# Leaky relu of the first block by ScalarE and GpSimd, VectorE in program order in the last four experts, gates copied by GpSimd

## The chip, the cores and the metric

The kernel runs on one core of a Trainium2 chip. The core has five engines, each with a queue of its own that it works off in order: TensorE (PE; its weight loads are shown apart as PEld), VectorE (DVE), ScalarE (ACT), GpSimd (POOL) and SyncE (SP), which here issues nearly all DMAs. The metric is the device time of one execution in microseconds, the median of several runs. Before the change it is 640.67 us (three runs, 638.81 to 641.47).

## The reference, cut to what matters

Three layers follow one another, on 2 x 768 = 1536 tokens of 512 features:

```python
scores = scale * q @ k.T; keep = is_sink | in_window      # 4 sinks, window 128, 8 heads of 64
x = softmax(where(keep, scores, -1e9)) @ v                # attention
h = x @ w_in                                              # [1536, 2048]; w_in, w_out are float64
x = maximum(0.01 * h, h) @ w_out                          # leaky relu layer
e = argmax(x @ w_gate); gate = softmax(x @ w_gate)[e]     # 8 experts, at most 384 tokens each
out[i] = gate[i] * (maximum(x[i] @ w1[e], 0) @ w2[e])     # w1: [8, 512, 1024], w2: [8, 1024, 512]
```

Tokens are queued for their expert in order, up to its capacity; the experts' weights come as float32. Products are made from high and low parts of float32 numbers, so each is three products on TensorE; only the first block of 256 tokens of the leaky relu layer is computed from whole float32 numbers in one pass.

## The kernel before, in words

**Attention and the leaky relu layer** are interleaved. The layer runs over six blocks j of 256 tokens, and in each over 16 chunks f of 128 hidden columns. For a chunk `first` (L832) makes the hidden product into a PSUM tile `hps`, `leak` (L847) takes it through the leaky relu into `g`, `split_g` makes high and low parts of it (not in block 0), and `second` (L867) multiplies it into the two output tiles `y`, two chunks later (LAG = 2). In block 0 there is one buffer for `hps`, so the next chunk's first product waits until the leaky relu has read the last one. Between the chunks run steps of attention for the tokens of later blocks, each of whose parts goes to an engine: exponentials on ScalarE (L213), their normalising on VectorE (L220, L221) and GpSimd (L223), the split of weights in high (ScalarE, L812) and low parts (GpSimd in block 0, L813), and so on.

In block 0 the float64 weights are also turned into float32, on VectorE, by three passes over integer words for each half of a chunk (`convert`, L767: lines 782, 786, 792).

The leaky relu before is two instructions: ScalarE writes 0.01 * h, VectorE takes the maximum of that and h. The tile `g` comes from a pool of three buffers. The pool named "c" holds 70 slots of 2 KB a partition for weights and attention's tiles.

**The experts** are ordered by their number of tokens, so that the last four have few. For one that has at most one tile of 128 tokens, `lone` (L1317) makes the two halves of the hidden layer (`up_one`), turns them and splits them (`turn_one`: high part on ScalarE, L1288, low part on VectorE, L1289), and multiplies down (`down`, L1291) into `py`, which VectorE multiplies by the gates (L1307) and GpSimd scatters to the output rows (L1308). Ahead of the last half's down product the next expert's tokens are turned and split by `turn_next` and `x_parts` (L1237), which also copies the gate and row number of each token from the loaded rows `xg` to `gt` (L1243). `fetch` loads the rows of the expert after the next. Between these, `refill(n)` converts n pieces of later experts' weights: a high part by ScalarE (L1142; 2 of 16 by VectorE, L1140) and a low part by VectorE (L1144). The numbers of pieces in `lone` are 4, 2, 5, 2, 3, in the order in which the calls stand.

**Order.** All engines but VectorE issue in the order in which the program traces them (`ORDERED`, L24, in force from L1459 on). VectorE's order is drawn up by a planner at build time, from priorities and estimated times; the conversions of block 0 are traced at a lower priority. The last four experts stand in one conditional block (L1419), which is taken when none of them has more than 128 tokens.

Of the kernel before, what the change touches and what calls it, by code (L numbers as in the profile page):

```python
# [8 lines left out]
F32 = mybir.dt.float32  # L9
F32R = mybir.dt.float32r  # L10
BF16 = mybir.dt.bfloat16
I32 = mybir.dt.int32
AF = mybir.ActivationFunctionType
ALU = mybir.AluOpType
# [4 lines left out]
P = 128  # L19
# [3 lines left out]
ET = mybir.EngineType  # L23
ORDERED = {ET.PE, ET.SP, ET.Activation, ET.Pool}  # L24
# [699 lines left out]
class FFN:  # L724
# [10 lines left out]
    N = 256  # L735
# [111 lines left out]
    def leak(self, j, f):  # L847

        nc, N = self.nc, self.N
        ps = self.g[j, f]  # L850
        g = self.p["g"].tile([P, N], F32, tag="g", name="g")
        nc.scalar.activation(g, ps, AF.Copy, scale=0.01)  # L852
        nc.vector.tensor_tensor(out=g, in0=ps, in1=g, op=ALU.max)  # L853
        self.g[j, f] = g

    def split_g(self, j, f, end=False):
# [204 lines left out]
class Experts:  # L1061
# [175 lines left out]
    def x_parts(self, gi, n, px):  # L1237

        nc, DM = self.nc, self.DM
        h, l = (self.xt[:, a, :, n * P:(n + 1) * P] for a in range(2))  # L1240
        nc.scalar.copy(h, px)
        nc.vector.tensor_tensor(out=l, in0=px, in1=h.bitcast(F32), op=ALU.subtract)  # L1242
        nc.vector.tensor_copy(self.gt[gi % 4][n].bitcast(I32), self.xg[gi % 2][n][:, DM:DM + 2].bitcast(I32))  # L1243

    def up(self, e, h, f, u0, u1):

# [141 lines left out]
    def run(self):  # L1388
        while len(self.w) < self.nchunk // 2:
            self.convert()  # L1390
        names = ("nout", "w", "raw", "free_raw", "free_w", "todo_load", "todo_conv", "nconv")

        def arms(gi, n):

            e, js = self.groups[gi]
            at = {a: getattr(self, a) for a in names}
            copy = lambda v: v if isinstance(v, int) else v.copy()
            for a in names:
                setattr(self, a, copy(at[a]))
            u0 = 1 if gi == 0 else 0  # L1400
            if n == u0:
                self.group(gi, n, u0)
                return
            with self.tc.If(self.cnt[e] > js[n - 1] * P) as c:
                self.group(gi, n, u0)
            for a in names:
                setattr(self, a, at[a])
            with c.Else():
                arms(gi, n - 1)

        tail = [gi for gi, (e, js) in enumerate(self.groups) if e >= self.short]
        for gi in range(tail[0]):
            arms(gi, len(self.groups[gi][1]))
        at = {a: getattr(self, a) for a in names}
        for a in names:
            setattr(self, a, at[a] if isinstance(at[a], int) else at[a].copy())
        with self.tc.If(self.cnt[self.E] <= P, preferred_fallthrough_block=True) as c:  # L1419
            for gi in tail:  # L1420
                if self.groups[gi][1][0] == 0 and self.NH == 2:
                    self.lone(gi, self.fetch_one)
                else:
                    self.group(gi, int(self.groups[gi][1][0] == 0), 0)
        for a in names:
            setattr(self, a, at[a])
        with c.Else():
            for gi in tail:
                arms(gi, len(self.groups[gi][1]))


def build(tc, A, n_sink, window, capacity):
# [14 lines left out]
    with ExitStack() as es:  # L1447
# [150 lines left out]
        for j in range(NB):  # L1598
# [9 lines left out]
            for i, f in enumerate(ffn.order(j)):  # L1608
# [6 lines left out]
                if ndone < min(count, count * (i + 1) // (ffn.NF - 1)):  # L1615
                    step(leak)
                    ndone += 1
                else:
                    leak()
# [104 lines left out]
```

## Time and profile before

| | |
|---|---|
| median of three runs | 640.67 us (638.81 to 641.47) |
| profiled execution | 638.71 us, span of its instructions 637.0 us, mean granted clock 0.991 |
| busy in the span | PE 594.7 us, DVE 431.0, ACT 342.6, POOL 232.9 |
| leaky relu, L852 and L853 over all six blocks | 96 instructions each, 0.380 and 0.419 us |
| last four experts | from 573.7 us to the end |

The profiler records one execution. Times are microseconds from the span's start. "Busy" counts an engine's instructions; an "idle before" or a bracket behind a timeline's row gives how long the engine stood still ahead of it and whose end it waited for. Matmul ends are modelled, so a busy TensorE is not TensorE at its peak. The granted clock is a share of full speed.

### The profile page before, as it was taken

The page shows a single profiled execution, that of the slowest core. Times are in us where ns is not written, and L with a number is a line of the kernel's source. Part 1 is how long each engine was busy: PE and PEld are TensorE (multiplying, and loading weights), DVE is VectorE, ACT ScalarE, POOL GpSimd, SP SyncE. Part 2 cuts the span into 40 slices and gives each one's busy share as a digit, 9 for nine tenths or more (in the row PEclk, how much of TensorE's full clock was granted, in tenths as well). Part 3 has the DMA queues.
Part 4 walks back from the last instruction along what each step waited for, and adds up shares of the span by engine and source line. Part 5 has one row for each costly group of instructions (what it writes and reads, how often), then busy time and mean ns, then how long its engine had stood idle before and what let it go on. Part 6 is the DMA issues. An engine that isn't in the chain of part 4 may idle for free.

```text
span 637.0 us, 12451 instructions
## 1 busy us (share of the span) xinstructions
PE 594.7 (93%) x4057; PEld 519.4 (82%) x4057; DVE 431.0 (68%) x1047; ACT 342.6 (54%) x997; POOL 232.9 (37%) x451
## 2 busy tenths in 40 slices
PE   8569888899999999999999999998999999997995
PEld 7457666679999999998999998986798888985774
DVE  5998999579976676667666662377466666556971
ACT  4546655777856566646665543264343444435741
POOL 5725556654464445535543453131101001010030
PEclk9988999999999999999999999999999999999999
DMA  8668889521445402140214006666257665437800
GB/s 240 160 201 244 267 221 288 154 84 51 176 145 169 127 17 69 38 139 8 62 32 132 2 31 209 218 206 196 92 166 232 215 201 177 150 120 225 278 14 13
DMA packets 83711, 91.83 MB, mean 144 GB/s; under 512 B 43171, under 2 KB 51363, under 8 KB 83616
## 3 DMA queue, kind: packets, MB, share of 16 engines
q1 hardware_dynamic: 81536, 85.58, 44.9%
q0 software_dynamic: 2080, 5.13, 2.2%
q8 instruction: 41, 0.67, 0.5%
q14 instruction: 54, 0.44, 0.2%
HBM read 71.91 MB, written 20.48 MB: 145 GB/s over the span
## 4 chain that ended last, share of the span: by engine, by line
PE 63%; DVE 17%; issue 10%; DMA 4%; ACT 4%; POOL 1%; another core or an unknown queue 0%; DVEq 0%; POOLq 0%; ACTq 0%
PE hps L844 16%; PE y L882 15%; PE py L1299 9%; PE ph L1252 8%; PE ops L300 4%; DMA out<-ys,gt 3%; DVE cvt L792 3%; PE sps L526 2%; DVE word L786 2%; DMA craw<-in_moe_w 2%; DVE word L782 2%; DVE g L853 1%; PE lps L965 1%; DVE cvt L786 1%; PE ph L1272 1%
## 5 line engine op out<-in xcount | busy, mean ns | idle before, releaser
L882 PE MATMUL y<-wh,gp 128*128 128x512 f32 x320 | 115.1, 400 | 1.4 <-ACT gp L862 1.4
L864 POOL TENSOR_TENSOR gp<-g,gp 128x256 fp32r<-128x256 f32 x77 | 56.8, 738 | 141.9 <-ACT gp L862 132.0
L844 PE MATMUL hps<-xth,wh 128*128 128x256 f32 x320 | 92.7, 290 | 0.0
L844 PE MATMUL hps<-xtl,wh 128*128 128x256 f32 x320 | 90.2, 282 | 0.0
L844 PE MATMUL hps<-xth,wl 128*128 128x256 f32 x320 | 90.0, 281 | 0.0
L1144 DVE TENSOR_TENSOR cw<-craw,cw 128x512 fp32r<-128x512 f32 x128 | 83.5, 697 | 8.7 <-ACT cw L1142 7.4
L1299 PE MATMUL py<-cw,ht 128*128 128x512 f32 x336 | 84.0, 403 | 4.5 <-DVE ht L1289 4.5
L1299 PEld LDWEIGHTS py<-cw,ht 128*128 128x128 f32 x336 | 63.0, 192 | 19.8 <-DVE ht L1289 6.2
L1142 ACT CAST cw<-craw 128x512 fp32r<-128x512 f32 x112 | 63.5, 621 | 28.1 <-PE py L1299 27.4
L1308 POOL DMA_INDIRECT out<-ys,gt x14 | 17.4, 1242 | 160.9 <-DVE ys L1307 146.5
L853 DVE TENSOR_TENSOR g<-hps,g 128x256 f32<-128x256 f32 x96 | 40.3, 419 | 52.4 <-ACT g L852 44.0
L852 ACT ACTIVATE g<-hps 128x256 f32<-128x256 f32 x96 | 36.4, 380 | 70.1 <-PE hps L844 70.0
L882 PEld LDWEIGHTS y<-wh,gp 128*128 128x128 f32 x320 | 60.0, 188 | 12.6 <-ACT gp L862 2.2
L844 PEld LDWEIGHTS hps<-xth,wh 128*128 128x128 f32 x320 | 60.3, 188 | 3.4 <-DVE g L853 0.7
L844 PEld LDWEIGHTS hps<-xtl,wh 128*128 128x128 f32 x320 | 60.3, 188 | 2.9 <-issue 0.5
L882 PE MATMUL y<-wl,gp 128*128 128x512 f32 x160 | 62.7, 392 | 0.0
L844 PEld LDWEIGHTS hps<-xth,wl 128*128 128x128 f32 x320 | 60.6, 189 | 0.0
L1252 PE MATMUL ph<-xt,cw 128*128 128x256 f32 (+2 forms) x444 | 58.2, 291 | 1.4 <-DVE xt L1242 0.9
L1252 PEld LDWEIGHTS ph<-xt,cw 128*128 128x128 f32 x444 | 56.6, 189 | 2.2 <-DVE xt L1242 1.6
L862 ACT CAST gp<-g 128x256 fp32r<-128x256 f32 x80 | 32.7, 409 | 39.0 <-DVE g L853 31.6
L213 ACT ACTIVATE pm<-pm,mx 128x132 f32<-128x132 f32 (+1 forms) x80 | 31.7, 398 | 30.7 <-DVE mx L539 30.4
L844 PE MATMUL hps<-xth,cvt 128*128 128x256 f32 x128 | 34.3, 415 | 8.2 <-DVE g L853 8.2
(205 smaller groups left out, 1282.0 us busy)
## 6 DMA issues: line engine op xcount, KB each, us to landing
craw<-in_moe_w SPq DMA_DIRECT2D x128, 256.0 KB
rawi<-in_moe_w_in SPq DMA_DIRECT2D x16, 512.0 KB
rawo<-in_moe_w_out SPq DMA_DIRECT2D x16, 512.0 KB
places<-zero SPq DMA_DIRECT2D x24, 257.0 KB
wh<-wscr SPq DMA_DIRECT2D x16, 256.0 KB
wl<-wscr SPq DMA_DIRECT2D x16, 256.0 KB
xg<-places SPq DMA_DIRECT2D x14, 257.0 KB
natv<-in_v SPq DMA_DIRECT2D x12, 256.0 KB
```

The lines of the kernel that those rows point to most:

```text
L213: nc.scalar.activation(pm[:, e, 0:w], pm[:, e, 0:w], AF.Exp, bias=mx[:, e:e + 1], accum_out=su[:, e:e + 1])
L300: nc.tensor.matmul(ps[:, e, :], lhsT=l, rhs=r, start=(x == 0), stop=(x == len(mm) - 1))
L844: nc.tensor.matmul(ps, lhsT=w, rhs=x, start=(n == 0), stop=(n == len(mm) - 1))
L852: nc.scalar.activation(g, ps, AF.Copy, scale=0.01)
L853: nc.vector.tensor_tensor(out=g, in0=ps, in1=g, op=ALU.max)
L862: nc.scalar.copy(gp[:, 0], g)
L864: eng.tensor_tensor(out=gp[:, 1], in0=g, in1=gp[:, 0].bitcast(F32), op=ALU.subtract)
L882: nc.tensor.matmul(y, lhsT=l, rhs=r, start=(start and n == 0), stop=(stop and n == len(mm) - 1))
L1142: nc.scalar.copy(h, t)
L1144: eng.tensor_tensor(out=l, in0=t, in1=h.bitcast(F32), op=ALU.subtract)
L1252: nc.tensor.matmul(self.ph[f][:, sl], lhsT=w, rhs=self.xt[:, a, k, sl], start=(m == 0), stop=(m == 3 * self.K - 1), skip_group_check=True)
L1299: nc.tensor.matmul(self.py[n], lhsT=x, rhs=w, start=(h == 0 and f == 0 and m == 0), stop=(h == self.NH - 1 and f == self.HF - 1 and m == 2))
```

## The change

In block 0 (j = 0) the leaky relu is computed as relu(h) - relu(-0.01 h): two activations by ScalarE, from PSUM to the two halves of a tile of the pool "c", and a subtraction by GpSimd into the first half. The other blocks keep the old form. In `x_parts` the copy of the gates goes from VectorE to GpSimd, in all experts. In the block of the last four experts VectorE, too, issues in the order of the program.

```diff
@@ leak
-        g = self.p["g"].tile([P, N], F32, tag="g", name="g")
-        nc.scalar.activation(g, ps, AF.Copy, scale=0.01)
-        nc.vector.tensor_tensor(out=g, in0=ps, in1=g, op=ALU.max)
+        if j == 0:
+            t = self.p["c"].tile([P, 2, N], F32, tag="c", name="gr")
+            g, r = t[:, 0], t[:, 1]
+            nc.scalar.activation(g, ps, AF.Relu)
+            nc.scalar.activation(r, ps, AF.Relu, scale=-0.01)
+            nc.gpsimd.tensor_tensor(out=g, in0=g, in1=r, op=ALU.subtract)
+        else:
+            g = self.p["g"].tile([P, N], F32, tag="g", name="g")
+            nc.scalar.activation(g, ps, AF.Copy, scale=0.01)
+            nc.vector.tensor_tensor(out=g, in0=ps, in1=g, op=ALU.max)
@@ x_parts
-        nc.vector.tensor_copy(self.gt[gi % 4][n].bitcast(I32), self.xg[gi % 2][n][:, DM:DM + 2].bitcast(I32))
+        nc.gpsimd.tensor_copy(self.gt[gi % 4][n].bitcast(I32), self.xg[gi % 2][n][:, DM:DM + 2].bitcast(I32))
@@ run
-            for gi in tail:
-                if self.groups[gi][1][0] == 0 and self.NH == 2:
-                    self.lone(gi, self.fetch_one)
-                else:
-                    self.group(gi, int(self.groups[gi][1][0] == 0), 0)
+            with self.tc.manual_schedule(engines=ORDERED | {ET.DVE}):
+                for gi in tail:
+                    if self.groups[gi][1][0] == 0 and self.NH == 2:
+                        self.lone(gi, self.fetch_one)
+                    else:
+                        self.group(gi, int(self.groups[gi][1][0] == 0), 0)
```

## Rows read from the trace of the kernel before

**Rows 1.** The page, busy time of each engine (share of span) and instructions:

```profile
PE 594.7 (93%) x4057; PEld 519.4 (82%) x4057; DVE 431.0 (68%) x1047; ACT 342.6 (54%) x997; POOL 232.9 (37%) x451
```

**Rows 2.** Busy times by stretch: length, engines (instructions), clock, DMA share, GB/s

```profile
42.37:114.34 71.97, 59.94 (x341) 43.43 (x341) 65.14 (x142) 43.42 (x139) 40.23 (x69) 0.98 0.91 257
114.34:131.75 17.41, 17.41 (x105) 12.81 (x104) 8.98 (x24) 10.80 (x35) 12.27 (x20) 1.00 0.30 96
```

**Rows 3.** Chain of waits in 42.37 to 114.34, shares by engine and line:

```profile
by line: DVE cvt L792 19.0%; DVE word L786 17.0%; DVE word L782 13.4%; issue 11.0%; PE hps L844 5.1%; ACT pm L213 4.9%; DVE pm L538 4.9%; DVE g L853 4.1%; DVE ri L220 2.9%; DVE xtl L311 2.9%; DVE mx L539 2.6%; ACT qT L193 2.0%; DVE qT L196 
```

**Rows 4.** Timeline of VectorE: start, duration, line, operation, operands [idle before]

```profile
48.07 0.16 DVE L220 TENSOR_SCALAR ri<-su 128x2 f32<-128x2 f32 x1
...
106.72 0.42 DVE L853 TENSOR_TENSOR g<-hps,g 128x256 f32<-128x256 f32 x1
107.06 0.68 DVE L792 SCALAR_TENSOR_TENSOR cvt<-rawi,word 128x512 int32<-128x512 int32 x1
```

**Rows 5.** Timeline of TensorE, fifth and sixth expert:

```profile
573.73 4.35 PE L1272 MATMUL ph<-cw,xt 128*128 128x512 f32 x18
...
588.08 3.88 PE L1299 MATMUL py<-cw,ht 128*128 128x512 f32 x10 [3.99 <-DVE ht L1289]
591.80 4.37 PE L1272 MATMUL ph<-cw,xt 128*128 128x512 f32 x18
...
602.38 2.60 PE L1299 MATMUL py<-cw,ht 128*128 128x512 f32 x10 [0.25 <-DVE ht L1289]
604.82 4.37 PE L1272 MATMUL ph<-cw,xt 128*128 128x512 f32 x18
```

**Rows 6.** Busy times by stretch, fifth and sixth expert:

```profile
573.73:591.80 18.07, 14.08 (x62) 11.07 (x61) 13.11 (x24) 10.40 (x20) 1.31 (x1) 0.91 0.73 229
591.80:604.82 13.02, 12.77 (x62) 10.11 (x60) 11.92 (x21) 9.69 (x20) 1.17 (x1) 1.00 0.87 289
```

**Rows 7.** Timeline of VectorE, fifth expert:

```profile
584.82 0.17 DVE L1243 COPY gt<-xg 128x2 int32<-128x2 int32 x1 [4.72 <-DMA xg<-places]
...
587.34 0.69 DVE L1289 TENSOR_TENSOR ht<-ph,ht 128x512 fp32r<-128x512 f32 x1
```

**Rows 8.** Groups of VectorE, 42.3 to 114.3: count | busy, mean ns | idle before

```profile
L792 DVE SCALAR_TENSOR_TENSOR cvt<-rawo,word 128x512 int32<-128x512 int32 x12 | 8.3, 688 | 0.3
...
L853 DVE TENSOR_TENSOR g<-hps,g 128x256 f32<-128x256 f32 x12 | 5.0, 419 | 1.2 <-ACT g L852 1.2
...
L220 DVE TENSOR_SCALAR ri<-su 128x2 f32<-128x2 f32 x8 | 3.2, 402 | 3.4 <-ACT pm L213 3.4
```

**Rows 9.** Waits in 42 to 114: us in total, times, longest

```profile
ACT pm L213 <- DVE mx L539: 11.6, 7, 3.6
...
PE hps L844 <- DVE g L853: 8.2, 5, 3.4
```

**Rows 10.** Groups of ScalarE over the span, shapes kept apart:

```profile
L1261 ACT ACTIVATE ht<-ph 128x256 fp32r<-128x256 f32 x24 | 9.3, 386 | 20.0 <-PE ph L1252 19.6 <-ACT cw L1142 0.5
...
L640 ACT ACT_TABLE_LOAD x1 | 1.3, 1283 | 0.8 <-PEq L1705 0.8
```

**Rows 11.** The page, costliest groups, GpSimd's subtraction in blocks 1 to 5:

```profile
L864 POOL TENSOR_TENSOR gp<-g,gp 128x256 fp32r<-128x256 f32 x77 | 56.8, 738 | 141.9 <-ACT gp L862 132.0
```

**Rows 12.** Timeline of all engines, 87 to 118, GpSimd beside VectorE:

```profile
100.42 1.26 POOL L813 TENSOR_TENSOR wl<-cvt,wh 128x512 fp32r<-128x512 f32 x1 [0.19 <-ACT wh L812]
100.58 1.13 DVE L220 TENSOR_SCALAR ri<-su 128x2 f32<-128x2 f32 x1
```

**Rows 13.** Timeline of VectorE, sixth expert:

```profile
595.93 1.29 DVE L1144 TENSOR_TENSOR cw<-craw,cw 128x512 fp32r<-128x512 f32 x2 [0.78 <-ACT cw L1142]
597.32 0.69 DVE L1289 TENSOR_TENSOR ht<-ph,ht 128x512 fp32r<-128x512 f32 x1
...
601.64 0.69 DVE L1289 TENSOR_TENSOR ht<-ph,ht 128x512 fp32r<-128x512 f32 x1
...
606.18 0.75 DVE L1307 TENSOR_SCALAR ys<-py,gt 128x512 f32<-128x512 f32 x1
```

## The prediction

> **What bounds the kernel now.** The page's busy times come first: TensorE works 93% of the span [rows 1], so the places to look for are those where it stands still or is fed late. Two of them touch this change.
>
> The first is block 0 of the leaky-relu layer. Read the busy time of each engine from the first leaky relu in block 0 (42.37 us) to the thirteenth (114.34 us): of 71.97 us VectorE is busy 65.14, TensorE 59.94, ScalarE 43.42, GpSimd 40.23 [rows 2]. The chain of waits over the same stretch lies nearly all on VectorE, half of it on the three lines that turn float64 weights into float32 (L782, L786, L792) [rows 3]. The timeline of VectorE shows the reader one instruction behind another, the max of the leaky relu among them [rows 4]. So VectorE sets the pace here, 71.97/12 = 6.0 us for each of twelve chunks. In the next stretch, 114.34 to 131.75, the last four chunks take 17.41/4 = 4.35 us each, with TensorE busy all the time and VectorE half of it [rows 2]: TensorE sets that pace, and there VectorE's work is covered.
>
> The second place is the fifth expert. TensorE's timeline gives the starts of the fifth, sixth and seventh, which have one tile of tokens each: 573.73, 591.80, 604.82 us [rows 5]. The fifth takes 18.07 us, the sixth 13.02, with the same work. In the fifth, TensorE waits 3.99 us for the low part of the hidden layer (DVE ht, L1289) and then needs 3.88 us for ten products that take 2.60 us in the sixth [rows 5]; the granted clock of that expert is 0.91, of the sixth 1.00 [rows 6]. VectorE's timeline says why: the copy of the gates (L1243) stands in its queue ahead of that low part, and waits 4.72 us for the token rows of a later expert to land; the low part starts at 587.34 [rows 7].
>
> **The change part by part.** All sums are against the profiled execution: 638.71 us, of which the span is 637.0. The median of the three runs is 640.67, 1.96 us more; I carry that over at the end.
>
> *The max leaves VectorE (block 0).* Removed: 16 instructions of L853. In the stretch that VectorE bounds there are 12, of 0.419 us each [rows 8]; but they overlap their neighbours, and from the start of one (106.72) to the start of the next instruction is 0.34 us [rows 4]. So 12 x 0.34 = 4.1 us come off the engine that sets the pace. In 2 cases VectorE also stood waiting for ScalarE's half of the leaky relu, 1.2 us in all [rows 8]; that goes too. The last four are under TensorE's work and I count them at nothing. What is late next: at 5.5 us a chunk VectorE is still slower than the 4.35 us that TensorE needs, so TensorE doesn't take the gain; only more than 12 x (6.0 - 4.35) = 20 us could meet that floor.
>
> *The product's buffer is given back earlier.* It is single in block 0, and TensorE waited 8.2 us in the window for the max to free it [rows 9]. After the change it waits for the second relu instead. Since VectorE sets the pace, I count this at nothing (ends: 0, and a gain of 5.6 us, which is all of VectorE's other idle time, 71.97 - 65.14 less the 1.2 above; a quarter of it, 1.4, goes into the range, since the chain puts a good part down to issue gaps, 11.0% of the stretch [rows 3]).
>
> *The second relu on ScalarE.* The trace of before has no relu in this stage; the nearest is the experts' L1261 of the same shape, 0.386 us [rows 10]. 12 x 0.39 = 4.6 us lift ScalarE to 48 of some 67 us. What hides it: ScalarE's exponentials wait 11.6 us in the window for VectorE's maximum [rows 9], so ScalarE is early where VectorE needs it. Counted at nothing; ends 0 and a loss of the full 4.6. Exp, Copy and Relu all run in this execution after a single table load [rows 10], so alternating them adds no load.
>
> *The subtraction on GpSimd.* Nearest row: gp of L864, same shape and engine, 0.738 us [rows 11]. 12 x 0.74 = 8.9 us on an engine busy 40.23 of 71.97. Its result is read two chunks later, some 9 to 11 us, so its own latency is covered; in GpSimd's order everything behind it in the step depends on ScalarE instructions that stand behind the relus anyway. The cost comes through VectorE: L220 takes 0.16 us alone [rows 4], but 1.13 when it starts at 100.58 while GpSimd's L813 runs from 100.42 to 101.68 [rows 12], and over the stretch its mean is 0.402 [rows 8]: 8 x 0.24 = 1.9 us lost now to 40.2 us of GpSimd work. Another 8.9 us in proportion is 0.4 us. Ends: 0, and the full 8.9 us if each subtraction held up VectorE for all its length. I take 0.4, from the row.
>
> *A slot of the common pool per chunk.* Up to three more of the 70 slots are held. By the code's counts, weights hold 3i+9 slots after chunk i up to 42, and 46 at the end; with some 21 for attention that is 63 to 67, so it fits, barely, at the end of the block. Counted at nothing; the other end is a rival below.
>
> Block 0 together: 4.1 + 1.2 - 0.4 = 4.9; I take 4.5, since VectorE's order is the planner's and will be redrawn. Everything behind block 0 is paced by TensorE and moves forward with it.
>
> *Gates copied by GpSimd, and VectorE in the order of the program in the last four experts.* Removed from VectorE: the copy, 0.17 us, and with it the 4.72 us wait [rows 7]. On GpSimd it stands after the next expert's transposes and before this expert's scatter; what is queued behind it is only that scatter, which needs the end of VectorE's output, later by all of the expert's last ten products [rows 5]. In the earlier experts the copy costs VectorE 0.17 us off the path: nothing. What is the order of the program? Read in lone(): six conversions, low part 0, five conversions, low part 1, two, the next tokens' low part, three, the output. The sixth expert already runs so: low part 0 at 597.32 behind the sixth conversion, low part 1 at 601.64 [rows 13]. There TensorE waits only 0.25 us [rows 5]. So the fifth should become like the sixth: 18.07 - 13.02 = 5.05 us, of which 1.28 is the slow clock behind the long wait. One thing is late next: VectorE is busy 11.92 of 13.02 us in the sixth expert [rows 6], so its backlog carries on; the end of the sixth expert's output comes 1.2 us behind TensorE's next expert (ys at 606.18, TensorE at 604.82) [rows 5, 13]. I take 0.45 off for that: 4.6. Ends: 2.0 and 5.3 (both short waits gone as well).
>
> **Sum.** 638.71 - 4.5 - 4.6 = 629.6 by the profiled execution; with the 1.96 us by which the median lies above it, 631.6. I forecast 631.5.
>
> **The rivals.**
>
> *Block 0 gives nothing, the tail gives all.* What VectorE saves is lost by GpSimd holding it up: half of the 8.9 us would eat the 4.9. For it: L220's stretch in rows 12, and 21 instructions of VectorE in the stretch (L220, L221, L176, L148) that work from SBUF alone. Against it: the present price is 1.9 us for 40 us. Time: 640.67 - 4.6 = 636.1. The Trainium skill has a rule for it (SBUF — State Buffer, section "SBUF: two separate sides"): VectorE and GpSimd take a shared port pair as an exclusive lock, held for the whole instruction, by a VectorE instruction with two SBUF inputs or in a two-port mode against a GpSimd one. The trace agrees: L220 ends at 101.71, just behind L813's end at 101.68 [rows 12]; by that rule the subtractions can take back anything up to their own 8.9 us.
>
> *The tail's wait is replaced.* In the order of the program VectorE can't step past a conversion whose weights or slot are late, and the low part of the fifth expert would stand behind it. For it: VectorE waited 0.78 us on such a conversion in the sixth [rows 13]. Against: that expert runs in that order and costs TensorE 0.25 us [rows 5]. With 4 us lost again, only block 0 and 0.6 us remain: 640.67 - 5.1 = 635.6.
>
> *Slower: the pool runs out.* The new tile comes from the pool of 70 slots, and ScalarE, in fixed order, would hold everything behind a leaky relu without a slot until a chunk later frees one: up to 4.35 us each [rows 2]. In the last four chunks that is 17.4 us lost against 9.1 gained: 640.67 + 8.3 = 649. It turns the sign from 9.1/4.35 = 2.1 such waits on. For it: the count above comes to 70 at the end. Against: conversions take slots from the same pool in this stretch and wait for none (0.3 us of idle time before the twelve of L792 from w_out) [rows 8].
>
> *The change doesn't do what it says:* the gates' copy was put down as waiting for the rows, but if low part 1 waited for something else as well, and block 0 also gave nothing, the time stays at 640.
>
> **How the numbers follow.** Chances: forecast 0.65 (its own range 628.5 to 634.5), block 0 nothing 0.15, tail replaced 0.10, slower by the pool 0.06, no change 0.04. The lower end of the range is both upper bounds (4.1 + 1.2 + 1.4, and 5.3), 640.67 - 12.0 = 628.7, and for runs nearer to the profiled execution's level 1.7 lower: 627. The upper end takes in both single-gain rivals: 637.5. A measurement of this kernel can tell about 0.5%, 3.2 us. Faster by more than that (under 637.5): 0.65 + 0.13 + 0.07 = 0.85; within: 0.09; slower: 0.06.
>
> **What would show it.** Right: from the first to the thirteenth chunk's relu some 67 us instead of 72; no DVE row of L853 in block 0, and no wait of TensorE for it; GpSimd subtractions near 0.74 us; L220's mean not far above 0.40. In the tail, the fifth expert at 13 to 13.5 us with granted clock 1.00 and waits of TensorE for L1289 below 0.5 us; L1243 on GpSimd behind the transposes. Wrong: L220 and L176 stretched to half a microsecond more in most chunks; ScalarE waiting for a slot ahead of a relu; a wait of some microseconds before a low part in the tail. A gain that shows in block 0 and not at the first product of block 1 would mean that TensorE, not VectorE, had bound it.

## The result and the profile after

The changed kernel took 631.58 us, the median of four runs (631.36 to 633.15), beside 639.75 for the kernel before on the same chip (four runs, 638.81 to 641.47): a ratio of 0.9875, with a 95% interval of 0.9845 to 0.9904. The forecast was 631.5. The profiled execution of the new kernel is the slowest of its four: 633.15 us, span 631.4; that of before took 638.71, span 637.0. So the two traces differ by 5.6 us and the medians by 8.2; the 1.54 us below is one piece of what lies between.

Six distances show where the time went; the table reads them off the timelines of TensorE and VectorE, in us. "Conversions of block 0" runs from the start of VectorE's first conversion by way of the PSUM tile `word` (L782 from w_in) to the start of its last (L792 from w_out). The 24 conversion passes ahead of it go straight to SBUF and are not in it.

| distance | before | after | change |
|---|---|---|---|
| conversions of block 0 | 73.56 | 70.79 | -2.77 |
| from there to block 1's first product | 15.68 | 15.68 | 0 |
| between the two halves of the router's logits | 4.67 | 6.21 | +1.54 |
| fifth expert of the tail | 18.07 | 13.01 | -5.06 |
| sixth, seventh expert | 13.02, 13.05 | 13.02, 13.01 | -0.04 |
| last expert's first product to the end of the span | 19.13 | 19.93 | +0.80 |

Every other distance differs by under 0.3 us. The 0.80 at the end lies behind the last scatter; an experiment below is about it.

**Block 0.** The page of the new kernel first, to be read beside [rows 1]: VectorE has 30 instructions fewer and GpSimd 30 more (16 of the leaky relu, 14 copies of gates), ScalarE 16 more.

```profile
PE 596.9 (95%) x4057; PEld 520.3 (82%) x4057; DVE 425.4 (67%) x1017; ACT 345.8 (55%) x1013; POOL 244.6 (39%) x481
```

Busy times by stretch, from that first conversion to the last and from there to block 1's first product (length; TensorE, its weight loads, VectorE, ScalarE, GpSimd with instruction counts; granted clock, DMA share, GB/s). Before:

```profile
40.18:113.74 73.56, 61.55 (x345) 44.53 (x344) 66.62 (x146) 43.25 (x138) 39.63 (x68) 0.97 0.90 255
113.74:129.42 15.68, 15.66 (x89) 11.17 (x89) 9.58 (x23) 10.98 (x35) 11.12 (x20) 1.00 0.38 117
```

After:

```profile
40.15:110.94 70.79, 61.73 (x346) 44.15 (x344) 64.00 (x133) 46.20 (x151) 48.01 (x80) 0.99 0.93 264
110.94:126.62 15.68, 15.65 (x89) 11.24 (x89) 8.03 (x19) 11.85 (x39) 12.86 (x22) 1.00 0.39 120
```

VectorE still has the most work, and the stretch shrank by about what its busy time lost, 2.62 us; its idle time hardly changed (6.94 us before, 6.79 after). The second stretch kept its 15.68 us, so the whole 2.8 us arrives at block 1.

What stands behind it is in the groups of VectorE and GpSimd over the new stretch (count | busy, mean ns | idle before). The maxima are gone; L220's mean went down against [rows 8], from 402 to 246 ns, and L176, whose mean before was 417 ns, went up to 758:

```profile
L176 DVE SCALAR_TENSOR_TENSOR qs<-natq,qs 128x256 fp32r<-128x256 f32 x4 | 3.0, 758 | 0.0
L220 DVE TENSOR_SCALAR ri<-su 128x2 f32<-128x2 f32 x8 | 2.0, 246 | 4.1 <-ACT pm L213 4.1
...
L857 POOL TENSOR_TENSOR gr<-gr 128x256 f32<-128x256 f32 x12 | 8.7, 729 | 10.5 <-ACT gr L856 10.5
```

The waits in 42 to 111 us (us in total, times, longest), for [rows 9]: TensorE's products now wait 1.7 us for the second relu, where they waited 8.2 for the max. As VectorE's idle time stayed what it was, I read the gain as its busy time and not as these 6.5 us.

```profile
ACT pm L213 <- DVE mx L539: 14.9, 4, 4.2
...
PE hps L844 <- ACT gr L856: 1.7, 2, 1.4
```

**The tail.** TensorE's timeline, fifth to seventh expert, for [rows 5]; and the stretch of the fifth, for [rows 6]:

```profile
572.43 4.35 PE L1280 MATMUL ph<-cw,xt 128*128 128x512 f32 x18
...
583.01 2.60 PE L1307 MATMUL py<-cw,ht 128*128 128x512 f32 x10 [0.25 <-DVE ht L1297]
585.44 4.37 PE L1280 MATMUL ph<-cw,xt 128*128 128x512 f32 x18
...
598.46 4.37 PE L1280 MATMUL ph<-cw,xt 128*128 128x512 f32 x18
```

```profile
572.43:585.44 13.01, 12.76 (x61) 10.12 (x60) 11.79 (x20) 9.70 (x20) 1.60 (x2) 1.00 0.69 220
```

The wait of 3.99 us is 0.25 and the clock of the expert is 1.00. GpSimd's timeline shows its two kinds of work there; the copy of the gates starts right behind the scatter of the previous expert and nothing waits for it:

```profile
573.72 1.21 POOL L1316 DMA_INDIRECT out<-ys,gt  x1 [4.60 <-DVE ys L1315]
574.92 0.40 POOL L1251 COPY gt<-xg 128x2 int32<-128x2 int32 x1
587.96 1.17 POOL L1316 DMA_INDIRECT out<-ys,gt  x1 [12.64 <-DVE ys L1315]
```

**The router.** The two halves of the logits (L973) in the new kernel's TensorE timeline, and the busy times of that stretch:

```profile
440.82 1.06 PE L973 MATMUL lps<-wg,x2T 128*128 128x8 f32 x8
442.80 0.18 PE L1004 MATMUL pps<-roh,before 128*128 128x8 bf16 x1 [0.92 <-DVE rsl L988]
...
447.03 0.98 PE L973 MATMUL lps<-wg,x2T 128*128 128x8 f32 x8
```

```profile
441.40:445.40 4.00, 3.08 (x17) 2.56 (x17) 2.03 (x15) 0.83 (x3) 0.47 (x1) 0.78 0.09 32
445.40:449.40 4.00, 4.00 (x20) 3.29 (x18) 1.46 (x9) 0.63 (x3) 0.72 (x2) 0.79 0.10 37
```

The change touches nothing here, and the same 0.92 us wait stands in the trace of before. But in this execution TensorE's granted clock is 0.78 and 0.79 in the mean over the two stretches behind it (part of each at the lower of its two levels, 1.2 and 2.4 GHz), and the distance is 1.54 us longer.

### The profile page after: what moved, and what is told of

It reads as the page before. It is cut to its first block, busy times and chain, and to the rows that moved or that the text cites. A ratio compares the mean times of both kernels' runs of the same rounds, so it can differ in the third digit from the quotient of the medians.

```text
span 631.4 us, 12497 instructions
## 1 busy us (share of the span) xinstructions
PE 596.9 (95%) x4057; PEld 520.3 (82%) x4057; DVE 425.4 (67%) x1017; ACT 345.8 (55%) x1013; POOL 244.6 (39%) x481
## 5 line engine op out<-in xcount | busy, mean ns | idle before, releaser
L1316 POOL DMA_INDIRECT out<-ys,gt x14 | 14.3, 1018 | 155.1 <-DVE ys L1315 155.1
L861 DVE TENSOR_TENSOR g<-hps,g 128x256 f32<-128x256 f32 x80 | 33.5, 419 | 48.7 <-ACT g L860 40.3
L860 ACT ACTIVATE g<-hps 128x256 f32<-128x256 f32 x80 | 30.3, 378 | 47.9 <-PE hps L844 47.8
L300 PE MATMUL ops<-pt,vt 128*64 128x128 f32 x456 | 38.9, 227 | 2.6 <-POOL pt L574 2.2
```

The lines of the kernel that those rows point to most:

```text
L300: nc.tensor.matmul(ps[:, e, :], lhsT=l, rhs=r, start=(x == 0), stop=(x == len(mm) - 1))
```

## The experiments

The first theory: two parts, each with its own gain, as in the prediction: block 0 saves VectorE's time less what GpSimd costs, and the tail saves the wait of a copy. The rivals: the subtraction eats the gain of block 0; and in the tail it is the order, or the copy's move, alone that counts. Ratios are against the kernel before, run beside each. Edits are shown against the changed kernel, unless a comment says otherwise.

**e1_leak: block 0's part alone.** The copy stays on VectorE, and the planner orders the tail.

```
-        nc.gpsimd.tensor_copy(self.gt[gi % 4][n].bitcast(I32), ...)
+        nc.vector.tensor_copy(self.gt[gi % 4][n].bitcast(I32), ...)
...
-            with self.tc.manual_schedule(engines=ORDERED | {ET.DVE}):
...
+            for gi in tail:
```

> The leaky relu's part of the change alone (two relus by ScalarE, subtraction by GpSimd, in block 0); the tail as before. Theory: the two parts are independent, and block 0 gives what the trace of the changed kernel shows at block 1's first max, 131.75 - 129.12 = 2.6 us: about 637.1 us, fifth expert still 18 us long. Rival, the prediction's own size: 4.5 us, 635.2 us.

Measured: 637.3 us, ratio 0.9963 (0.994 to 0.9985): the theory's 637.1 and not the rival's 635.2. The conversions of block 0 took 70.78 us; the fifth expert 18.77, with the old wait at its place in VectorE's timeline, and TensorE's wait behind it:

```profile
582.54 0.17 DVE L1251 COPY gt<-xg 128x2 int32<-128x2 int32 x1 [4.80 <-DMA xg<-places]
585.06 0.68 DVE L1297 TENSOR_TENSOR ht<-ph,ht 128x512 fp32r<-128x512 f32 x1
```

```profile
585.79 4.64 PE L1307 MATMUL py<-cw,ht 128*128 128x512 f32 x10 [3.94 <-DVE ht L1297]
```

So the 2.77 us of block 0 belong to this part and to nothing else.

**e2_gates and e3_order: the two edits of the tail, one at a time.** Both keep the old leaky relu.

```
# e2_gates, against before
-        nc.vector.tensor_copy(self.gt[gi % 4][n].bitcast(I32), ...)
+        nc.gpsimd.tensor_copy(self.gt[gi % 4][n].bitcast(I32), ...)
# e3_order, against before
+            with self.tc.manual_schedule(engines=ORDERED | {ET.DVE}):
```

> The gates' copy by GpSimd alone; VectorE still in the planner's order, leaky relu as before. Theory: the wait of 4.72 us goes with the copy, whatever the order: fifth expert at 13.0 us, 634.7 us in all. Rival: the order is what counts, and the planner's order keeps another wait ahead of the low part: fifth expert over 15 us, 637 us or more.

> VectorE in program order in the last four experts alone; the copy of the gates stays on VectorE. Theory: in program order the copy stands behind both low parts, and the rows that it needs have landed by then: fifth expert at 13.0 to 13.3 us (0.17 us for each copy, at most), 634.8 us. Rival: the copy waits for rows wherever it stands on VectorE: fifth expert at 17 us or more, 639 us.

Measured: e2_gates 635.36 us, 0.9928 (0.9903 to 0.9953); e3_order 633.6, 0.9898 (0.9857 to 0.9939). The fifth expert takes 13.00 us in the one and 13.06 in the other. TensorE, e2_gates:

```profile
573.32 4.35 PE L1272 MATMUL ph<-cw,xt 128*128 128x512 f32 x18
...
583.89 2.59 PE L1299 MATMUL py<-cw,ht 128*128 128x512 f32 x10 [0.26 <-DVE ht L1289]
586.32 4.37 PE L1272 MATMUL ph<-cw,xt 128*128 128x512 f32 x18
```

VectorE, e3_order: the copy has moved from ahead of the low part to behind it and behind the next tokens' low part, and by then its rows have landed, so it waits for nothing.

```profile
586.97 0.68 DVE L1289 TENSOR_TENSOR ht<-ph,ht 128x512 fp32r<-128x512 f32 x1
588.76 0.69 DVE L1242 TENSOR_TENSOR xt<-px,xt 128x512 fp32r<-128x512 f32 x1
589.37 0.16 DVE L1243 COPY gt<-xg 128x2 int32<-128x2 int32 x1
```

Either edit alone brings the whole tail; they don't add up. The fault was one instruction at one place in one queue, and taking it out or moving it back mends it. With the old leaky relu the conversions of block 0 took 73.51 us in e2_gates and 74.36 in e3_order. In the latter the maxima waited 2.2 us for ScalarE instead of 1.2, and the mean granted clock of the stretch was 0.95 instead of 0.97.

**e4_nosub: without the subtraction.** If GpSimd's 8.7 us hold VectorE up, taking them out should show it. The kernel leaves out the negative side of the leaky relu in block 0.

```
             nc.scalar.activation(r, ps, AF.Relu, scale=-0.01)
-            nc.gpsimd.tensor_tensor(out=g, in0=g, in1=r, op=ALU.subtract)
```

> The changed kernel without GpSimd's subtraction in block 0 (the leaky relu's negative side is left out there, both relus are still made). Theory: the subtraction holds up L176 and L148 on VectorE, which cost 1.6 us more per step than before the change; that comes back in part: block 1's first max 0.5 to 1.5 us earlier than at 129.12, about 630.5 us in all. Rival, the lock for the subtraction's full length: 4 us or more earlier, under 628 us. Rival, no part of the loss is GpSimd's: 129.1, 631.6 us.

Measured: 634.18 us, 0.9906 (0.9875 to 0.9937), and a conversion stretch of 71.34 us, not shorter than 70.79. My theory of 0.5 to 1.5 us back fell. (It was stated for block 1's first max, which came at 129.94 us instead of 129.12; but here TensorE's clock fell behind the conversions, as shown in the last section, so the stretch is the better measure.) The groups of VectorE say why, beside the rows of after above: L176 is down to 508 ns, 1.0 us less in all, but L220 has risen from 246 to 414, 1.3 us more.

```profile
L220 DVE TENSOR_SCALAR ri<-su 128x2 f32<-128x2 f32 x8 | 3.3, 414 | 4.1 <-ACT pm L213 4.1
L176 DVE SCALAR_TENSOR_TENSOR qs<-natq,qs 128x256 fp32r<-128x256 f32 x4 | 2.0, 508 | 0.0
```

Which of VectorE's instructions meets which of GpSimd's is a matter of their places. In the timeline of after only three of the seven held-up instructions stand beside a subtraction (one L176, two L220); in e4_nosub two of the L220 stand beside an L813 instead and take 1.12 and 1.18 us.

**e5_dvemax: the max put back as an extra.** All of the change stays, and VectorE does the old max into a buffer that nobody reads. That is the price of the maxima without the subtraction's. The max reads `hps` again, too, so TensorE's products wait for it as before (6.7 us, as against 8.2 and 1.7).

```
+            x = self.p["g"].tile([P, N], F32, tag="g", name="gx")
+            nc.vector.tensor_tensor(out=x, in0=ps, in1=r, op=ALU.max)
             nc.gpsimd.tensor_tensor(out=g, in0=g, in1=r, op=ALU.subtract)
```

> The changed kernel with one maximum of the old form (128x256 from PSUM and SBUF) put back on VectorE per chunk of block 0, its result unused. Measured is the stretch of VectorE from the first conversion into the PSUM word to the last one of block 0: 73.56 us before the change, 70.79 after. Theory: the maxima filled gaps between conversions that wait for one another, which are bare after the change, so putting them back costs less than their own 12 x 0.34 = 4.1 us: about 2.8 us more, 73.6, and with waits for the relus up to 74.5. Rival, the prediction's step: 4.1 us and the waits of 1.2 us, 76.1. In all 635 us against 637.

Measured: 636.64 us, 0.9935 (0.99 to 0.9969); the stretch is 73.95 us, 3.16 more than after. The twelve maxima, by start to start, take 4.0 us and have waits of 1.1 before them (the next group), as in the kernel before; yet the stretch grew by 3.16, which is nearer to the theory's 2.8 than to the 5.3 of the prediction's step.

```profile
L858 DVE TENSOR_TENSOR gx<-hps,gr 128x256 f32<-128x256 f32 x12 | 5.0, 417 | 1.1 <-ACT gr L856 1.0
```

Added up from start to start, the rest is in two places. Conversions, masks and reductions, with their waits, take 1.1 us less when the maxima stand between them. L176, L148 and L220 take 0.9 us less: they are held up less by GpSimd at their new places. The first of the two can be seen in the timelines. VectorE in e5_dvemax:

```profile
106.10 0.69 DVE L786 SCALAR_TENSOR_TENSOR word<-rawi,word 128x512 int32<-128x512 int32 x1
106.70 0.42 DVE L858 TENSOR_TENSOR gx<-hps,gr 128x256 f32<-128x256 f32 x1
107.04 0.68 DVE L792 SCALAR_TENSOR_TENSOR cvt<-rawi,word 128x512 int32<-128x512 int32 x1
```

and in after, the same two conversions of another chunk with nothing between:

```profile
84.67 0.70 DVE L786 SCALAR_TENSOR_TENSOR word<-rawi,word 128x512 int32<-128x512 int32 x1
85.40 0.69 DVE L792 SCALAR_TENSOR_TENSOR cvt<-rawi,word 128x512 int32<-128x512 int32 x1
```

L792 reads what L786 wrote, and starts 0.73 us behind it. The max needs nothing from L786 and starts 0.60 behind it, overlapping its end; L792 comes 0.34 later. From L786 to L792 that is 0.94 us with the max and 0.73 without: there a max costs 0.21 us, not 0.34.

**e7_noeps: without L220.** A last test of what GpSimd's work costs: L220, the instruction most held up before, is left out, with its addition of 1e-9 to the softmax's sums.

```
-        nc.vector.tensor_scalar(out=ri, in0=su, scalar1=1.0e-9, scalar2=None, op0=ALU.add)
-        nc.vector.reciprocal(ri, ri)
+        nc.vector.reciprocal(ri, su)
```

> The changed kernel without L220 on VectorE: the 1e-9 added to a softmax sum of at least 1, which float32 doesn't hold. Theory: in block 0 VectorE sets the pace, so the eight L220 of the stretch give back their 1.87 us less what the reciprocal then waits for GpSimd in their place (0.5 us or so): the stretch goes from 70.79 to about 69.4 us, 630.2 us in all against 631.6. Rival: what held up L220 now holds up the reciprocal for as long, and the wait for ScalarE moves to it: 70.5 or more, 631.4 us.

Measured: 632.12 us (630.79 to 634.96), 0.9856 (0.9808 to 0.9903), not told apart from a_again below. The theory fell: VectorE's busy time drops from 64.00 to 62.68 us and the stretch stays, at 70.91.

```profile
39.80:110.71 70.91, 61.96 (x346) 44.77 (x344) 62.68 (x125) 46.35 (x151) 48.10 (x80) 0.97 0.92 260
```

The reciprocal now stands where L220 stood, with the same waits for ScalarE's exponential, and new short ones came elsewhere:

```profile
55.33 0.17 DVE L220 RECIPROCAL ri<-su 128x2 f32<-128x2 f32 x1 [1.01 <-ACT pm L213]
...
72.52 0.58 DVE L310 TENSOR_TENSOR xtl<-ops,xth 64x128 fp32r<-64x128 f32 x2 [0.25 <-ACT xth L304]
```

So 1.3 us less of VectorE's work isn't 1.3 us less of the stretch: its idle time grew from 6.79 to 8.23 us, so by now part of the pace is set by what VectorE waits for. The rival had the time right (70.5 or more) and not the reason: the reciprocal, with 0.16 us, is not held up.

**a_again: the changed kernel once more,** unedited, beside the last two.

> The changed kernel once more, to stand beside the others on one chip: stretch 70.8 us, 631.6 us, with executions near 633 where TensorE's clock is granted at the lower level around 441 to 449 us.

Measured: 633.26 us (632.65 to 634.55), 0.9878 (0.9832 to 0.9923). The conversions took 70.76 us. In all five traces with the new block 0 unedited they take 70.76 to 70.79, and in the three with the old one 73.51 to 74.36, so the gain is no accident of one trace. But here the stretch from the last conversion to block 1 took 17.37 us where after's took 15.68, at a granted clock of 0.90:

```profile
110.57:127.94 17.37, 17.35 (x88) 11.85 (x89) 8.02 (x19) 11.85 (x39) 12.90 (x22) 0.90 0.40 113
```

**e9_dve_copy and b_again: the end of the span.** From the end of the last scatter's issue on GpSimd to the end of the span it is 4.9 us in before, 4.5 in e1_leak and 4.8 in e3_order, and 5.7 in after, 5.5 to 5.8 in the four other kernels named above that copy the gates on GpSimd, 5.7 in a_again. So the copy was put back on VectorE, with the order kept, and the changed kernel run beside it.

```
-        nc.gpsimd.tensor_copy(self.gt[gi % 4][n].bitcast(I32), ...)
+        nc.vector.tensor_copy(self.gt[gi % 4][n].bitcast(I32), ...)
```

> The changed kernel with the copy of the gates back on VectorE, and VectorE in program order in the last four experts as in the change: block 0's part and the order, without GpSimd's copy. Asked because in all traces with the copy on GpSimd the span ends 5.5 to 5.8 us after the last scatter's issue, and in all three without it 4.5 to 4.9. Theory (the copy on GpSimd costs at the end): 4.5 to 4.9 us after the last scatter, the fifth expert at 13.1 as in e3_order, block 0's conversions at 70.8, and a median about 0.9 us under that of the changed kernel beside it, within what a run can tell. Rival (the end differs by accident, or hangs on something else of the change): 5.5 to 5.8 us after the last scatter and the same median. A second rival: the copy on VectorE delays the low part of an expert with early rows; then TensorE waits over 0.3 us for it in the tail.

> The changed kernel unedited, beside e9_dve_copy. Both theories: 631 to 634 us, conversions of block 0 at 70.8 us, fifth expert 13.0, and the span's end 5.5 to 5.8 us after the last scatter's issue.

Measured: e9_dve_copy 632.32 us (631.85 to 632.98), 0.9872 (0.9845 to 0.99); b_again 632.1 (631.4 to 634.1), 0.9872 (0.9842 to 0.9901). The last scatter in e9_dve_copy, whose span is 631.26, and in b_again, whose span is 632.28:

```profile
625.82 0.98 POOL L1316 DMA_INDIRECT out<-ys,gt  x1 [11.06 <-DVE ys L1315]
```

```profile
625.27 0.97 POOL L1316 DMA_INDIRECT out<-ys,gt  x1 [11.04 <-DVE ys L1315]
```

4.5 us in the one and 6.0 in the other: eleven traces now divide by where the copy is, 4.5 to 4.9 on VectorE and 5.5 to 6.0 on GpSimd. The rows of the program's last line show which instruction differs, GpSimd's closing DRAIN, the longest of three (shortest, median and longest in ns; first and last start). In e9_dve_copy and in b_again:

```profile
L1730 POOLq DRAIN  x3: 51/107/3333, 626.9 to 631.0; - x3
```

```profile
L1730 POOLq DRAIN  x3: 51/107/2277, 629.2 to 632.0; - x3
```

With the copy on VectorE (four traces) the DRAIN starts 0.1 us behind the scatter's issue and ends 1.1 us behind the landing of the scatter's rows. With the copy on GpSimd (seven traces) it starts only about when those rows land, 2.4 to 2.9 us behind the issue, and then takes 2.28 us. Why the copy has this effect no run shows. Conversions (70.78 and 70.79) and fifth expert (13.01 in both) don't differ, nor does the copy hold up a low part. But the medians are the same, so the 0.7 us or more at the end is shown in the traces and not in the times. It is no faster version.

## Why the prediction was right, and where its terms were off

**The bound of block 0: right.** The prediction said that VectorE sets the pace and that a gain would therefore reach block 1. The gain of 2.77 us in the conversions is 2.80 us at block 1's first product, and e5_dvemax takes it back with the maxima. There TensorE waits for the max again as well, so this run alone doesn't part the two; that VectorE lost 2.62 us of busy time and 0.15 of idle time does. The prediction's own sign, some 67 us from the first chunk's relu to the thirteenth's instead of 72 (from max to max), is less firm: from relu to relu it is 70.7 us before and 68.1 in after, but 69.6 in a_again and b_again, since the first relu's start moves (41.80, 39.97 and 40.44 us). The chain of [rows 3] puts about two thirds of the stretch on lines of VectorE and 11.0% on issue, not nearly all on VectorE, as the prediction read.

**The gain of block 0: 4.5 forecast, 2.77 measured.** The step that was mis-sized is "12 x 0.34 = 4.1 us come off the engine that sets the pace". The 0.34 was the right distance, but on the wrong pair: it ends at the next instruction and ignores that the max had filled a gap that its neighbours leave when they stand together. VectorE's instructions, added up start to start over both stretches, with idle time on rows of its own or with the instruction behind it, give the account in us:

| | change |
|---|---|
| maxima gone, start to start | -4.0 |
| their waits for ScalarE gone | -1.2 |
| gaps that open at conversions (+0.82), masks (+0.32) and reductions (+0.19) | +1.3 |
| held up beside GpSimd: L176 +1.39, L148 +0.19, L220 -1.15 | +0.4 |
| waits of L220 for ScalarE's exponential, 3.45 to 4.05 | +0.6 |
| all others | +0.1 |
| sum | -2.8 |

The term for the waits (1.2) held. That for GpSimd (0.4) held in size, but by luck: it was taken from L220, which got shorter, and the loss came at L176 and L148. The gaps were not in the prediction. Nor was the last term, the waits of L220: that they come from the two relus in ScalarE's queue is likely, and no run separates it.

**The rival of the port: half of it seen, and small.** The prediction gave a chance of 0.15 to a loss of the whole gain. GpSimd's subtractions lasted 0.73 us as the row had it, and instructions of VectorE that meet GpSimd's are held up. In the timeline of after, L176, 0.417 us in the mean before, takes 0.64 beside a subtraction, and 0.97 beside L232, which is attention's.

```profile
45.92 0.73 POOL L857 TENSOR_TENSOR gr<-gr 128x256 f32<-128x256 f32 x1 [1.97 <-ACT gr L856]
46.29 0.64 DVE L176 SCALAR_TENSOR_TENSOR qs<-natq,qs 128x256 fp32r<-128x256 f32 x1
...
96.93 0.94 POOL L232 TENSOR_TENSOR pl<-pm,ph 128x264 fp32r<-128x264 f32 x1
97.18 0.97 DVE L176 SCALAR_TENSOR_TENSOR qs<-natq,qs 128x256 fp32r<-128x256 f32 x1
```

But the net price was 0.4 us of a possible 8.7, and neither taking the subtraction away nor taking L220 away shortened the stretch. The Trainium skill's rule (SBUF — State Buffer, section "SBUF: two separate sides") is that of a lock for a whole instruction. A single meeting looks like that here: L176 and L148 meet a running instruction of GpSimd five times in the stretch of after, and end 0.28 or 0.29 us behind its end each time, as in the two pairs above. The runs add that over this stretch the total hangs on which instructions meet, and not on GpSimd's busy time.

**The release of hps, the second relu and the slots: right at nothing.** The waits of TensorE's products for the buffer fell by 6.5 us without a gain of their own that the account would show, ScalarE took 3 us more work in the stretch, and no row shows an engine waiting for a slot of the pool. The rival of the pool did not occur.

**The tail: 4.6 forecast, 5.06 measured.** The mechanism was as told: the copy's wait of 4.72 us ahead of the low part, and the slow clock behind it. The 0.45 taken off for VectorE's backlog was not needed: the fifth expert became the sixth to within 0.01 us. The rival that another wait would take its place fell with e3_order, which has the feared order and 13.06 us. What the prediction did not say is that one of the two edits is enough, and it costed GpSimd's copy at nothing, where the traces show 0.8 us at the end of the span.

**The sum.** 2.77 + 5.06 = 7.8 us by the stages, less the 0.8 at the end, gives 7.0, beside a forecast of 9.1 and differences of the medians of 8.2, 7.1 (a_again) and 8.6 us (b_again). What lies between these is not accounted for; falls of the clock, as in the last section, are of that size. The forecast hit 631.58 to 0.1 us, but partly by luck: it stood on a median of 640.67, and the four runs of before now give 639.75; and the gain of block 0 was put 1.7 us too high, that of the tail 0.5 too low. The parts run alone gain 2.4 us (e1_leak), 4.4 (e2_gates) and 6.1 (e3_order, four runs that spread over 4.4 us) by their medians.

## What to carry to other kernels

An instruction taken off the bounding engine gives back the difference between the distances of its neighbours with and without it, not its own step: where the neighbours depend on each other, it had been filling a gap (0.21 us a max instead of 0.34). Before moving work between engines, look for a copy in a busy queue that waits for a transfer of a later stage; here either edit that took it out of the way was worth the whole wait, and the second one nothing. And after a small gain in a tight stage, expect the next saving there to be worth less, as with the 1.3 us of L220.

## What the runs showed of the hardware

TensorE's granted clock falls in some executions at a place where in others of the same kernel it doesn't. In after it was 1.00 from 110.94 to 126.62 us and 0.78 behind the router's wait; in a_again it was 0.90 at the first place, and the router's distance was 4.66 us. Of eleven profiled executions, six show the first fall (e3_order, e4_nosub, e5_dvemax, e7_noeps, a_again, e9_dve_copy; 1.6 to 2.1 us) and four the second (after, e3_order, e4_nosub, b_again; 1.1 to 1.5 us); before, e1_leak and e2_gates show neither. In e4_nosub, four products behind a wait for VectorE take 3.50 us, where four of the same take 1.93 later. The granted clock is 0.50 in the first stretch, the lower of TensorE's two levels (1.2 GHz beside 2.4), and 1.00 in the second:

```profile
110.20 0.73 PE L526 MATMUL sps<-kT,qT 128*128 128x264 f32 x3 [1.03 <-DVE qT L196]
110.73 3.50 PE L889 MATMUL y<-cvt,gr 128*128 128x512 f32 x4
...
116.64 1.93 PE L889 MATMUL y<-cvt,gr 128*128 128x512 f32 x4
```

Both places come behind waits of TensorE, as did the slow end of the fifth expert in before (0.91 in [rows 6]); but the same waits stand in executions where the clock stayed at 1.00. These falls are not small beside the 2.77 us of block 0, so the stages were compared by their own distances and not by the total. What decides whether an execution has one is open.
